# Block transposes on VectorE in place of TensorE transposes for six experts' tokens

## Chip, core and metric

The kernel runs on one core of one Trainium2 chip. The metric is the device time of one execution in microseconds, the lower the better. Of the core's engines five matter: TensorE (PE, matmuls, and PEld, its weight loads), VectorE (DVE), ScalarE (ACT), POOL, and SP, whose queue issues the loads of the weights. Each engine takes its instructions strictly in the order in which the program has them.

## The reference

```
state = alpha[t] * state + k[t] v[t]^T        # per batch (2) and head (8), 768 steps, 48 wide
y[t] = q[t] state                             # -> x, 1536 tokens x 384
# first layer: top-1 of 8 experts, capacity 384, F = 1024
x = gate * (relu(x_e @ w1[e]) @ w2[e])
# second layer: noisy top-2 of 8 experts, no capacity
for e in range(8):
    for k in range(2):
        mask = top2[:, k] == e
        h = relu(x[mask] @ moe2_w1[e])
        out[mask] += top2_w[mask, k] * (h @ moe2_w2[e])
```

All of it is in f32. An f32 product is made here from a high part and a rest of both factors, in three matmuls.

## The kernel before

A manual schedule writes every instruction out in the order of its engine. Sixteen jobs follow one another, one per expert: jobs 0 to 7 are the first layer, jobs 8 to 15 the second. Jobs 8 and 9 of the second layer are experts 0 and 1 (304 and 432 token places), jobs 10 to 15 the six others, called placed experts: which of them comes when is decided on the chip by their counts, and they have 432, 412, 400, 396, 384 and 384 places (CAPS). Their rows and weights are therefore addressed by a register.

A job n has two stages of eight steps f each. `hidden` (lines 600 to 615): per f six matmuls of the three 128-feature chunks of xh, the high part of the tokens (line 608), then three of xl, the rest (line 611); ScalarE and VectorE make h and its rest from PSUM (lines 613, 614). `second` (lines 619 to 637): per f nine matmuls (line 637) that build three output tiles py. Between them, at f = 2, 6 and 7 of `second`, stands `split_x` of the next job, one chunk d of its tokens each time: TensorE transposes the gathered rows (line 567, with the identity iw), ScalarE copies PSUM to xh (line 571), VectorE subtracts for xl (line 572). The stage `hidden` of the next job takes chunk d of xh with its matmuls 2d + 1 and 2d + 2.

`load_x` (line 551) gathers the rows of the next job on POOL's queue, each row of 394 f32: 384 features, then gate, token and others. They were put into the store xs2 by scatters at the end of the first layer.

The weights of the next job are loaded by SP (lines 490 for w1, 493 for w2), and split in sixteen parts q: ScalarE makes the high part (line 508), and the rest is a subtract with two SBUF inputs (line 509), which goes to POOL or to VectorE by a string, ENGS. In the second layer that string gives q = 11 and q = 14 to VectorE and the other fourteen to POOL; q = 8 to 15 stand between the steps f of `second`. (In job 9, q = 4 to 7 stand there too.)

At the end of a job ScalarE copies output tiles 0 and 2 to yT (line 813) and VectorE tile 1 (line 811); TensorE transposes yT back to rows after the next job's first f (line 821), these are weighted (lines 789, 791) and scattered by POOL into the output (line 157). Jobs 14 and 15 compute rows directly and have no yT.

Of the kernel before, what the change touches and what calls it, by code (L numbers as in the profile page):

```python
# [6 lines left out]
F32 = mybir.dt.float32  # L7
# [5 lines left out]
ALU = mybir.AluOpType  # L13
# [13 lines left out]
NF2 = 2  # L27
# [39 lines left out]
def body(tc, ap, cap, dbg=False, stop=False):  # L67
    nc = tc.nc
    V, A, G, PE = nc.vector, nc.scalar, nc.gpsimd, nc.tensor
    with ExitStack() as ctx:  # L70
# [124 lines left out]

        zt = []

        def zero_rows(store, e, n, r):

            nc.sync.dma_start(store[:E * R].rearrange("(e r) d -> r e d", e=E)[r:r + 128, e:e + n],  # L200
                              zt[0][:, None, :RW].to_broadcast([128, n, RW]))

        def zero_xs1():
            zero = s6([128, 1536])
# [5 lines left out]
        def zero_xs2():  # L210
            zero_rows(xs2, 0, 1, LOW3)
            zero_rows(xs2, 0, E, LOW2)

        def zero_out(i):
            nc.sync.dma_start(out[i * 512:(i + 1) * 512].rearrange("(p k) d -> p (k d)", p=128), zt[0][:, :4 * DM])
# [265 lines left out]
        def raw(n, i):  # L481
            if n >= len(jobs):
                return
            layer = jobs[n][0]
            e = expert(n, mybir.EngineType.SP)
            one = slice(e, e + 1) if place(n) is None else bass.ds(e, 1)
            w1, w2 = ap[f"w1_{layer}"][one], ap[f"w2_{layer}"][one]
            if i < 2:
                t = s6([128, ND, 512])
                nc.sync.dma_start(t, w1.rearrange("o (d p) f -> p (o d) f", p=128)[:, :, i * 512:(i + 1) * 512])  # L490
            else:
                t = s6([128, 4, DM])
                nc.sync.dma_start(t, w2.rearrange("o (f p) d -> p (o f) d", p=128)[:, (i - 2) * 4:(i - 1) * 4, :])
            raws[n, i] = t
# [27 lines left out]
            return hi[:, f % 4, :], lo[:, f % 4, :]  # L522


        xg, xsp = {}, {}

        def dims(n):

# [13 lines left out]
        def load_x(n, eng):  # L542
            layer, e = jobs[n]
            nt_, p, c = dims(n)
            store = (xs1, xs2)[layer - 1]
            g = sb([p, nt_, RW], "b6", 5)
            if place(n) is None:
                rows_ = store[e * R:e * R + nt_ * p]
            else:
                rows_ = store[bass.ds(expert(n, eng.engine) * R, nt_ * p), :]  # L550
            eng.dma_start(g, rows_.rearrange("(t p) d -> p t d", p=p))
            xg[n] = g
            xsp[n] = (xb([128, ND, c], F32R), xb([128, ND, c], F32R))

        def split_x(n, d):
            layer, e = jobs[n]
            nt_, p, c = dims(n)
            g, (xh, xl) = xg[n], xsp[n]
            ds = (d,)
            if layer == 1:  # L560
                if d == 2:
                    return
                ds = ((0, 1), (2,))[d]
            xp = pm()
            for k, d in enumerate(ds):
                for t, sl, r in tiles(n):
                    PE.transpose(xp[:, k * c + sl.start:k * c + sl.stop], g[:r, t, d * 128:(d + 1) * 128],  # L567
                                 ident[:r, :r])
            m = lambda x: x[:, ds[0]:ds[-1] + 1, :].rearrange("p d c -> p (d c)")
            w = len(ds) * c  # L570
            A.activation(m(xh), xp[:, :w], AF.Copy)  # L571
            V.tensor_tensor(m(xl), xp[:, :w], m(xh).bitcast(F32), op=ALU.subtract)  # L572
# [755 lines left out]
def prepare(i):  # L1328
# [13 lines left out]
    for (b, c0, n) in (a_ for ps_ in PARTS for a_ in ps_):  # L1342
# [11 lines left out]

    by_part = lambda x, n: x.reshape(n, 128, E).transpose(1, 0, 2)
    w2 = np.concatenate([by_part(i["moe2_w_gate"], ND), by_part(i["moe2_w_noise"], ND)], axis=2)
    few = np.concatenate([x.reshape(128, -1) for x in (wg1, w2, by_part(i["moe2_noise"], N // 128))], axis=1)

    return {
        "q": q[:, :HR], "k": k[:, :HR], "ks": of_pieces(k), "qs": of_pieces(q), "a": a[:, :HR], "few": few, "as": np.concatenate(pieces, axis=1),  # L1360
        "v": np.ascontiguousarray(i["v"].transpose(0, 2, 1, 3)).reshape(B, S, DM),
        "wgn": i["moe_w_gate"],
        "w1_1": i["moe_w1"], "w2_1": i["moe_w2"], "w1_2": i["moe2_w1"], "w2_2": i["moe2_w2"],
    }


# [15 lines left out]
```

## Time and profile before

| | us |
|---|---|
| median of 3 runs | 490.23 (489.21 to 491.54) |
| profiled execution, device time | 492.09 |
| its span | 490.2 |
| TensorE busy | 474.1 (97%) |
| VectorE busy | 308.4 (63%) |
| ScalarE busy | 262.6 (54%) |
| POOL busy | 319.9 (65%) |
| mean granted clock of TensorE | 0.993 |

The profile is of one execution; its device time lies 1.86 us over the median, and is 1.9 longer than its span. Busy shares are over all stages. The second layer takes the part of the span from about 267 on; job 9's `second` begins at 296.68, job 10's `hidden` at 311.93, and job 15's `hidden` at 456.56.

### The profile page before, as it was taken

How to read it: one execution, taken by the hardware profiler on the slowest of the kernel's cores; microseconds unless marked ns; L12 is line 12 of the kernel's file. 1: busy time of each engine (PE TensorE's matmuls, PEld its weight loads, DVE VectorE, ACT ScalarE, POOL GpSimd, SP SyncE). 2: the span in 40 equal slices, each digit the busy share in tenths (PEclk: the TensorE clock that was granted, in tenths of full speed). 3: DMA queues.
4: the chain of work that ended last, by engine and by line, in shares of the span. 5: the costliest groups of instructions: out<-in, count | busy, mean ns of one | idle time of the engine just before them, and what ended most of it. 6: DMA issues, size and time to landing. Idle time of an engine off the chain costs nothing.

```text
span 490.2 us, 9808 instructions
## 1 busy us (share of the span) xinstructions
PE 474.1 (97%) x3542; PEld 445.6 (91%) x3542; DVE 308.4 (63%) x856; ACT 262.6 (54%) x676; POOL 319.9 (65%) x400
## 2 busy tenths in 40 slices
PE   8899999999999999999999999999999999999993
PEld 4588888899999999999998799999999999999993
DVE  7989988557786786786863424735454362746540
ACT  3467787466666675675661356453535536354310
POOL 3434496565777777885865269695794949779322
PEclk9989999999999999999999999999999999999998
DMA  8953863699888868676733854482745847361133
GB/s 284 407 194 137 322 238 103 213 319 283 282 264 264 267 219 274 181 242 216 232 107 105 254 122 151 140 216 78 178 126 156 212 127 165 110 164 21 20 46 42
DMA packets 47797, 91.65 MB, mean 187 GB/s; under 512 B 4625, under 2 KB 29154, under 8 KB 47739
## 3 DMA queue, kind: packets, MB, share of 16 engines
q1 hardware_dynamic: 38090, 70.32, 43.2%
q0 software_dynamic: 9648, 20.61, 18.1%
q8 instruction: 30, 0.49, 0.4%
q14 instruction: 29, 0.23, 0.2%
HBM read 70.63 MB, written 20.28 MB: 185 GB/s over the span
## 4 chain that ended last, share of the span: by engine, by line
PE 68%; DVE 16%; DMA 4%; issue 4%; ACT 4%; POOL 3%; SPq 0%; POOLq 0%; DVEq 0%
PE py L637 28%; PE ph L608 18%; PE ph L611 9%; DMA xs<-b,m_si 3%; PE pm L567 2%; DVE s L509 2%; DVE s L236 2%; DVE h L614 2%; POOL xs L157 2%; PE pm L821 2%; DVE s L253 1%; DVE s L255 1%; PE pm L665 1%; DVE s L240 1%; PE pm L365 1%
## 5 line engine op out<-in xcount | busy, mean ns | idle before, releaser
L509 POOL TENSOR_TENSOR s<-s,s 128x384 fp32r<-128x384 f32 x175 | 184.6, 1263 | 50.1 <-ACT s L508 45.2
L637 PE MATMUL py<-h,s 128*128 128x240 f32 (+5 forms) x1008 | 154.3, 307 | 0.0
L637 PEld LDWEIGHTS py<-h,s 128*128 128x128 f32 x1008 | 142.7, 189 | 1.1
L608 PE MATMUL ph<-x,s 128*128 128x240 f32 (+6 forms) x768 | 136.0, 312 | 1.9 <-DVE h L614 0.9
L508 ACT ACTIVATE s<-s 128x384 fp32r<-128x384 f32 x256 | 123.1, 515 | 1.1 <-DMA s<-w 1.0
L608 PEld LDWEIGHTS ph<-x,s 128*128 128x128 f32 x768 | 115.5, 189 | 4.5 <-DVE h L614 2.5
L614 DVE SCALAR_TENSOR_TENSOR h<-ph,h 128x240 fp32r<-128x240 f32 (+6 forms) x128 | 61.1, 484 | 70.5 <-ACT h L613 63.8
L509 DVE TENSOR_TENSOR s<-s,s 128x384 fp32r<-128x384 f32 x81 | 88.3, 1111 | 3.4 <-ACT s L508 2.7
L613 ACT ACTIVATE h<-ph 128x240 fp32r<-128x240 f32 (+6 forms) x128 | 55.2, 432 | 59.9 <-PE ph L611 55.5
L611 PE MATMUL ph<-x,s 128*128 128x240 f32 (+6 forms) x384 | 76.6, 308 | 0.0
L157 POOL DMA_INDIRECT out<-b,m_ix x29 | 46.5, 1605 | 43.0 <-ACT b L789 23.0
L611 PEld LDWEIGHTS ph<-x,s 128*128 128x128 f32 x384 | 61.2, 189 | 0.4
L571 ACT ACTIVATE x<-pm 128x480 fp32r<-128x480 f32 (+7 forms) x38 | 18.6, 489 | 63.3 <-PE pm L567 63.3
L157 POOL DMA_INDIRECT xs<-b,m_si x32 | 32.9, 1028 | 16.4 <-DVE pm L746 11.4
L298 POOL TENSOR_SCALAR_AFFINE_SELECT h<-h 128x512 f32<-128x512 f32 x24 | 22.1, 942 | 30.8 <-ACT h L297 30.3
L572 DVE TENSOR_TENSOR x<-pm,x 128x480 fp32r<-128x480 f32 (+7 forms) x38 | 20.7, 550 | 27.6 <-ACT x L571 27.2
L637 PE MATMUL py<-s,h 128*128 128x384 f32 x144 | 26.5, 339 | 0.0
L637 PEld LDWEIGHTS py<-s,h 128*128 128x128 f32 x144 | 25.0, 188 | 0.0
L236 DVE TENSOR_TENSOR s<-s,s 112x256 f32<-112x256 f32 (+2 forms) x24 | 19.3, 824 | 1.6 <-DMA s<-qs 1.1
L567 PE MATMUL pm<-iw,b 108*128 108x108 f32 (+5 forms) x129 | 18.7, 260 | 0.8 <-DVE h L865 0.5
L155 POOL MEMSET spacer<- 1x1 f32 x74 | 18.8, 254 | 0.1
L169 PE MATMUL ph<-warm 128*128 128x512 bf16 x66 | 16.9, 415 | 1.5 <-POOL warm L164 1.5
(240 smaller groups left out, 553.9 us busy)
## 6 DMA issues: line engine op xcount, KB each, us to landing
s<-w SPq DMA_DIRECT2D x64, 768.0 KB, 5.7
xs<-s SPq DMA_DIRECT2D x2, 1576.0 KB, 6.5
out<-s SPq DMA_DIRECT2D x4, 768.0 KB, 8.2
b<-xs POOLq DMA_DIRECT2D x4, 664.9 KB
b<-xs POOLq DMA_DIRECT2D x7, 369.4 KB
s<-as SPq DMA_DIRECT2D x2, 780.5 KB
s<-ks SPq DMA_DIRECT2D x2, 768.0 KB, 9.0
s<-qs SPq DMA_DIRECT2D x2, 768.0 KB
```

What stands on the lines that cost most here:

```text
L157: st = G.indirect_dma_start(out=dst, out_offset=bass.IndirectOffsetOnAxis(ap=ix, axis=0), in_=src, in_offset=None, **kw)
L236: eng.tensor_tensor(o, src[:, h].rearrange("r (s j) -> r s j", j=64), x[:, h].rearrange("r (s j) -> r s j", j=64), op=ALU.mult)
L298: G.affine_select(a_, a_, pattern=[[0, 4], [1, 128]], compare_op=ALU.is_ge, fill=0.0, base=0, channel_multiplier=-1)
L508: A.activation(hi[sl], t[sl], AF.Copy)
L509: rest.append(lambda: (eng or V).tensor_tensor(lo[sl], t[sl], hi[sl].bitcast(F32), op=ALU.subtract))
L567: PE.transpose(xp[:, k * c + sl.start:k * c + sl.stop], g[:r, t, d * 128:(d + 1) * 128], ident[:r, :r])
L572: V.tensor_tensor(m(xl), xp[:, :w], m(xh).bitcast(F32), op=ALU.subtract)
L608: PE.matmul(p, w, x[:, d, :], start=(k == 0), stop=False)
L611: PE.matmul(p, w1_of(n, f, d)[0], xl[:, d, :], start=False, stop=(d == ND - 1))
L613: A.activation(hh, p, AF.Relu)
L614: V.scalar_tensor_tensor(hl, p, 0.0, hh.bitcast(F32), op0=ALU.max, op1=ALU.subtract)
L637: PE.matmul(out_, l, r, start=(f == 0 and k == 0), stop=(f == NF - 1 and k == 2))
```

## The change

For the six placed experts the features no longer come as whole rows. Four loads on SP's queue (line 570 of the changed kernel) bring blocks of 32 tokens by 96 features: block b of the features goes to partitions 32b to 32b + 31, so that token j of a group of 32 lies on partition 32b + j. VectorE then turns each chunk of 32 columns, 32 by 32 (line 583), into a tile y of 128 features by the tokens, rounded up to a multiple of 32. ScalarE makes xh from y (line 584), VectorE xl from y and xh (line 585), all in SBUF. Feature 96b + 32d + i becomes row 32b + i of chunk d, and the rows of the first weights are put in that order on the host (`by_block`, a new input w1_b). POOL's load (line 565) is left with the last ten columns. Rows of the store up to the next multiple of 32 are set to zero in the first layer. The order of the steps is left as it is: chunk d stands where chunk d stood. Line numbers shift: 490 and 493 become 491 and 494, 508 and 509 become 509 and 510, 608 and 611 become 635 and 638, 637 becomes 664, 811 and 813 become 838 and 840, 821 becomes 848.

```diff
--- before.py
+++ after.py
@@ -195,10 +195,10 @@
 
         zt = []
 
-        def zero_rows(store, e, n, r):
-
-            nc.sync.dma_start(store[:E * R].rearrange("(e r) d -> r e d", e=E)[r:r + 128, e:e + n],
-                              zt[0][:, None, :RW].to_broadcast([128, n, RW]))
+        def zero_rows(store, e, n, r, k=128):
+
+            nc.sync.dma_start(store[:E * R].rearrange("(e r) d -> r e d", e=E)[r:r + k, e:e + n],
+                              zt[0][:k, None, :RW].to_broadcast([k, n, RW]))
 
         def zero_xs1():
             zero = s6([128, 1536])
@@ -210,6 +210,7 @@
         def zero_xs2():
             zero_rows(xs2, 0, 1, LOW3)
             zero_rows(xs2, 0, E, LOW2)
+            zero_rows(xs2, NF2, E - NF2, C2, -C2 % 32)
 
         def zero_out(i):
             nc.sync.dma_start(out[i * 512:(i + 1) * 512].rearrange("(p k) d -> p (k d)", p=128), zt[0][:, :4 * DM])
@@ -484,7 +485,7 @@
             layer = jobs[n][0]
             e = expert(n, mybir.EngineType.SP)
             one = slice(e, e + 1) if place(n) is None else bass.ds(e, 1)
-            w1, w2 = ap[f"w1_{layer}"][one], ap[f"w2_{layer}"][one]
+            w1, w2 = ap[f"w1_{layer}" if place(n) is None else "w1_b"][one], ap[f"w2_{layer}"][one]
             if i < 2:
                 t = s6([128, ND, 512])
                 nc.sync.dma_start(t, w1.rearrange("o (d p) f -> p (o d) f", p=128)[:, :, i * 512:(i + 1) * 512])
@@ -522,7 +523,18 @@
             return hi[:, f % 4, :], lo[:, f % 4, :]
 
 
-        xg, xsp = {}, {}
+        xg, xsp, xr_ = {}, {}, {}
+
+        class few_of:
+
+            def __init__(self, x):
+                self.x, self.shape = x, (*x.shape[:2], RW)
+
+            def __getitem__(self, at):
+                p, t, c = at
+                if isinstance(c, slice):
+                    return self.x[p, t, c.start - DM:None if c.stop is None else c.stop - DM]
+                return self.x[p, t, c - DM]
 
         def dims(n):
 
@@ -543,12 +555,20 @@
             layer, e = jobs[n]
             nt_, p, c = dims(n)
             store = (xs1, xs2)[layer - 1]
-            g = sb([p, nt_, RW], "b6", 5)
             if place(n) is None:
-                rows_ = store[e * R:e * R + nt_ * p]
+                g = sb([p, nt_, RW], "b6", 5)
+                eng.dma_start(g, store[e * R:e * R + nt_ * p].rearrange("(t p) d -> p t d", p=p))
             else:
-                rows_ = store[bass.ds(expert(n, eng.engine) * R, nt_ * p), :]
-            eng.dma_start(g, rows_.rearrange("(t p) d -> p t d", p=p))
+                nb = -(-c // 32)
+                t6 = sb([128, nb * ND * 32 + nt_ * (RW - DM)], "b6", 5)
+                g = few_of(t6[:p, nb * ND * 32:].rearrange("p (t d) -> p t d", t=nt_))
+                eng.dma_start(g[:, :, DM:], store[bass.ds(expert(n, eng.engine) * R, nt_ * p), :].rearrange(
+                    "(t p) d -> p t d", p=p)[:, :, DM:])
+                x = xr_[n] = t6[:, :nb * ND * 32].rearrange("p (t d) -> p t d", t=nb)
+                rows_ = store[bass.ds(expert(n, mybir.EngineType.SP) * R, nb * 32), :]
+                for b in range(4):
+                    nc.sync.dma_start(x[b * 32:b * 32 + 32], rows_.rearrange("(t j) d -> j t d", j=32)[
+                        :, :, b * ND * 32:(b + 1) * ND * 32])
             xg[n] = g
             xsp[n] = (xb([128, ND, c], F32R), xb([128, ND, c], F32R))
 
@@ -557,6 +577,13 @@
             nt_, p, c = dims(n)
             g, (xh, xl) = xg[n], xsp[n]
             ds = (d,)
+            if place(n) is not None:
+                x = xr_[n][:, :, d * 32:d * 32 + 32]
+                y = hb([128, x.shape[1] * 32])
+                V.transpose(y.rearrange("p (t j) -> p t j", j=32), x)
+                A.activation(xh[:, d, :], y[:, :c], AF.Copy)
+                V.tensor_tensor(xl[:, d, :], y[:, :c], xh[:, d, :].bitcast(F32), op=ALU.subtract)
+                return
             if layer == 1:
                 if d == 2:
                     return
@@ -1354,13 +1381,14 @@
 
     by_part = lambda x, n: x.reshape(n, 128, E).transpose(1, 0, 2)
     w2 = np.concatenate([by_part(i["moe2_w_gate"], ND), by_part(i["moe2_w_noise"], ND)], axis=2)
+    by_block = i["moe2_w1"].reshape(E, 4, ND, 32, F).transpose(0, 2, 1, 3, 4).reshape(E, DM, F)
     few = np.concatenate([x.reshape(128, -1) for x in (wg1, w2, by_part(i["moe2_noise"], N // 128))], axis=1)
 
     return {
         "q": q[:, :HR], "k": k[:, :HR], "ks": of_pieces(k), "qs": of_pieces(q), "a": a[:, :HR], "few": few, "as": np.concatenate(pieces, axis=1),
         "v": np.ascontiguousarray(i["v"].transpose(0, 2, 1, 3)).reshape(B, S, DM),
         "wgn": i["moe_w_gate"],
-        "w1_1": i["moe_w1"], "w2_1": i["moe_w2"], "w1_2": i["moe2_w1"], "w2_2": i["moe2_w2"],
+        "w1_1": i["moe_w1"], "w2_1": i["moe_w2"], "w1_2": i["moe2_w1"], "w1_b": by_block, "w2_2": i["moe2_w2"],
     }
```

On VectorE, in job 9's `second`, behind the rests of its hidden layer, there stood before (x_4401 is xl of job 10, pm a transposed chunk, s weights of job 10):

```order
L572 TENSOR_TENSOR x_4401<-pm_4566,x_4400 128x432
L509 TENSOR_TENSOR s_846_4547<-s_821_4436,s_845_4546 128x384
L509 TENSOR_TENSOR s_848_4551<-s_777_4228,s_847_4550 128x3x128
L572 TENSOR_TENSOR x_4401<-pm_4628,x_4400 128x432
L572 TENSOR_TENSOR x_4401<-pm_4648,x_4400 128x432
L509 TENSOR_TENSOR s_852_4615<-s_838_4510,s_851_4614 128x384
L811 COPY b_856_4666<-py_4537 128x432
```

And there stands now, in the changed kernel (h_4571, h_4630 and h_4647 are the tiles y, b_810 the loaded blocks):

```order
L583 STREAM_TRANSPOSE h_4571<-b_810_4396 128x448
L585 TENSOR_TENSOR x_4406<-h_4571,x_4405 128x432
L510 TENSOR_TENSOR s_846_4552<-s_821_4441,s_845_4551 128x384
L510 TENSOR_TENSOR s_848_4556<-s_777_4229,s_847_4555 128x3x128
L583 STREAM_TRANSPOSE h_4630<-b_810_4396 128x448
L585 TENSOR_TENSOR x_4406<-h_4630,x_4405 128x432
L583 STREAM_TRANSPOSE h_4647<-b_810_4396 128x448
L585 TENSOR_TENSOR x_4406<-h_4647,x_4405 128x432
L510 TENSOR_TENSOR s_852_4617<-s_838_4515,s_851_4616 128x384
L838 COPY b_856_4662<-py_4542 128x432
```

Three transposes have come in, one ahead of each subtract for xl, and the subtract's first input has gone from PSUM (pm) to SBUF (h). Both L510 of q = 7 and q = 11 still stand behind the first subtract.

On TensorE, in the same place ahead of f = 7 of that `second`, there stood before (iw is the identity):

```order
L637 MATMUL py_4541<-h_4505,s_829_4471 128x432
L567 MATMUL pm_4648<-iw_83,b_810_4395 128x108 x4
L637 MATMUL py_4533<-h_4525,s_828_4470 128x432
L637 MATMUL py_4533<-h_4526,s_828_4470 128x432
L637 MATMUL py_4533<-h_4525,s_829_4471 128x432
```

The row of line 567 is gone after. At the end of the same `second` and the start of job 10's `hidden` there stands now:

```order
L664 MATMUL py_4546<-h_4530,s_829_4476 128x432
L635 MATMUL ph_4673<-x_4405,s_830_4479 128x432
L635 MATMUL ph_4673<-x_4405,s_831_4480 128x432
L635 MATMUL ph_4673<-x_4405,s_830_4479 128x432
L635 MATMUL ph_4673<-x_4405,s_831_4480 128x432
L635 MATMUL ph_4673<-x_4405,s_830_4479 128x432
L635 MATMUL ph_4673<-x_4405,s_831_4480 128x432
L638 MATMUL ph_4673<-x_4406,s_830_4479 128x432 x3
L848 MATMUL pm_4688<-iw_83,b_856_4662 108x128 x3
```

There is nothing left between the last matmul with w2 and the first of `hidden`, nor further ahead, that reads the tokens of job 10; the matmuls themselves stand as before. On SP's queue the four loads of line 570 stand behind the two w1 loads of the same job and ahead of its two w2 loads, for each of the six jobs.

## Rows read from the trace of the kernel before

**Rows 1.** The page, part 1: busy time, share and count of each engine.
```profile
PE 474.1 (97%) x3542; PEld 445.6 (91%) x3542; DVE 308.4 (63%) x856; ACT 262.6 (54%) x676; POOL 319.9 (65%) x400
```

**Rows 2.** Windows: stretch, length, busy time (instructions) by engine, granted clock, DMA share, GB/s.
```profile
core 0: us, PE busy (x) PEld busy (x) DVE busy (x) ACT busy (x) POOL busy (x), PEclk, DMA share, GB/s
312.00:342.70 30.70, 30.70 (x169) 29.18 (x168) 13.86 (x23) 14.38 (x31) 21.38 (x25) 1.00 0.64 173
```

**Rows 3.** Chain of waits, 296 to 457: shares by line, then pieces (start, us, what).
```profile
by line: PE py L637 50.2%; PE ph L608 28.0%; PE ph L611 14.1%; PE pm L821 4.1%; PE pm L567 3.9%
...
300.20 0.37 PE pm L567 x4
...
311.93 1.18 PE ph L608 x6
...
429.08 1.05 PE ph L608 x6
...
454.65 0.33 PE pm L567 x3
```

**Rows 4.** Groups by line and form, whole run: busy us, mean ns, idle before.
```profile
L572 DVE TENSOR_TENSOR x<-pm,x 128x432 fp32r<-128x432 f32 x6 | 3.4, 599 | 3.4 <-ACT x L571 3.3
L240 DVE TENSOR_TENSOR_SCAN s<-s,s 112x512 f32<-112x512 f32 x2 | 2.4, 1218 | 0.0
L571 ACT ACTIVATE x<-pm 128x432 fp32r<-128x432 f32 x6 | 3.2, 530 | 6.9 <-PE pm L567 6.9
L508 ACT ACTIVATE s<-s 128x384 fp32r<-128x384 f32 x256 | 123.1, 515 | 1.1 <-DMA s<-w 1.0
```

**Rows 5.** Timeline of POOL, job 9: start, us, instruction, idle before it, releaser.
```profile
291.43 18.74 POOL L509 TENSOR_TENSOR s<-s,s 128x384 fp32r<-128x384 f32 x19
```

**Rows 6.** Timeline of VectorE in the same stretch of job 9, and in job 10.
```profile
301.18 0.61 DVE L572 TENSOR_TENSOR x<-pm,x 128x432 fp32r<-128x432 f32 x1 [3.29 <-ACT x L571]
302.47 8.59 DVE L509 TENSOR_TENSOR s<-s,s 128x384 fp32r<-128x384 f32 x2 [0.69 <-POOL s L509]
...
332.71 3.92 DVE L509 TENSOR_TENSOR s<-s,s 128x384 fp32r<-128x384 f32 x1 [0.24 <-ACT s L508]
```

**Rows 7.** Timelines at the ends of jobs 10 and 13, POOL and VectorE.
```profile
341.95 1.01 POOL L509 TENSOR_TENSOR s<-s,s 128x384 fp32r<-128x384 f32 x1 [5.75 <-ACT s L508]
...
342.00 1.38 DVE L509 TENSOR_TENSOR s<-s,s 128x384 fp32r<-128x384 f32 x1
...
428.50 1.45 POOL L509 TENSOR_TENSOR s<-s,s 128x384 fp32r<-128x384 f32 x1 [3.32 <-ACT s L508]
...
428.52 0.55 DVE L509 TENSOR_TENSOR s<-s,s 128x384 fp32r<-128x384 f32 x1
...
429.46 0.51 DVE L766 TENSOR_SCALAR m_iz<-b 108x4 f32<-108x4 f32 x1
430.01 0.16 DVE L767 TENSOR_TENSOR m_iz<-m_iz,tro 108x4 f32<-108x4 f32 x1
```

**Rows 8.** Timeline of POOL, its streams in jobs 13 and 14.
```profile
415.71 9.47 POOL L509 TENSOR_TENSOR s<-s,s 128x384 fp32r<-128x384 f32 x9
...
443.74 9.25 POOL L509 TENSOR_TENSOR s<-s,s 128x384 fp32r<-128x384 f32 x9
```

**Rows 9.** Timeline of SP's queue, job 8: loads of job 10's weights.
```profile
267.88 1.13 SPq L490 DMA_DIRECT2D s<-w  x2
272.70 7.74 SPq L493 DMA_DIRECT2D s<-w  x2
```

**Rows 10.** Timelines of POOL and VectorE in the first layer.
```profile
179.39 3.28 POOL L509 TENSOR_TENSOR s<-s,s 128x384 fp32r<-128x384 f32 x3 [0.34 <-ACT s L508]
...
180.90 2.19 DVE L509 TENSOR_TENSOR s<-s,s 128x384 fp32r<-128x384 f32 x2
```

**Rows 11.** Timeline of TensorE at 24 us, and windows as in group 2.
```profile
24.15 0.57 PE L283 MATMUL py<-iw,s 112*128 112x112 f32 x4 [1.41 <-DVE s L236]
...
26.00:29.30 3.30, 3.30 (x18) 2.78 (x17) 3.23 (x4) 1.88 (x7) 2.72 (x3) 0.50 0.15 56
```

## The prediction

> **What bounds the kernel now.** I read the busy line first: TensorE works 97% of the span [rows 1]. That alone names no limit, so I cut the stretch of the second layer into windows: from 312.00 to 342.70 TensorE is busy for all 30.70 us at a granted clock of 1.00, VectorE for 13.86 and POOL for 21.38 [rows 2]. The chain of waits over jobs 9 to 14 consists of TensorE alone, and its line of shares gives the transposes of line 567, the only TensorE work that the change takes out there, 3.9% [rows 3]. So a transpose removed is time won, provided that what replaces it is ready before TensorE asks for it. The question is therefore how late VectorE is at the end of each `second`, and for that I read the timelines of POOL and VectorE side by side.
>
> **What is removed.** Six placed experts times three chunks are 18 pieces of line 567, the first of 0.37 us at 300.20 and the last of 0.33 at 454.65 [rows 3]. By width: 3 x 0.37 (432 tokens) + 0.36 + 0.36 + 0.35 (412) + 3 x 0.35 (400) + 3 x 0.34 (396) + 6 x 0.33 (384) = 6.2 us. This is the most the change can win.
>
> **What is added on VectorE and ScalarE.** Per chunk a block transpose T (line 583) comes new; the copy on ScalarE and the subtract S stay, but read the SBUF tile y instead of PSUM. The trace has no block transpose. From below, T costs what VectorE takes for one pass over 128x432, 0.60 us [rows 4]; from above, what a scan takes, whose 1.22 us for 512 columns [rows 4] is 1.07 for 448. I take 0.61: T makes one independent pass, as the subtract does, where a scan carries a value from column to column. That y is read from SBUF by ScalarE costs nothing extra: the copy takes 530 ns from PSUM for 432 columns, the weights' copy 515 from SBUF for 384 [rows 4], the same per column within a few per cent.
>
> **The wait that appears.** S now has two SBUF inputs, as the weights' subtract L509 has. In job 9 POOL runs L509 without a gap from 291.43 to 310.17 [rows 5]. VectorE's L509, asked for at 302.47, ends with a second one at 311.06 [rows 6]: two operations of 0.55 us each took 8.59, that is, the first got no turn before POOL's stream ended; in job 10 one alone took 3.92 [rows 6]. The L572 before it, with one input in PSUM, took 0.61 in the midst of the same stream [rows 6]. So after the change S for chunk 0 waits for the end of POOL's stream, P, in every job; and since VectorE takes its work in order, L510 (the old L509) and T and S for chunks 1 and 2 stand behind it, where before only chunks 1 and 2 stood behind L509, with their copies still to come from TensorE.
>
> From P on, VectorE and ScalarE take turns. Steps, with 0.08 us overlap of successive VectorE operations and 0.04 for a handover: S0 ends at P + 0.47; each L510 behind it adds 0.47 (two in job 9, one later); T1 0.53; the ScalarE copy 0.61; S1 0.64; T2 0.53; copy 0.61; S2 0.64.
>
> Job 9: P = 310.17, hence copy 1 at 312.72, copy 2 at 314.50, S2 at 315.14. Without its three transposes TensorE would start `hidden` of the next job 1.11 earlier than 311.93 [rows 3], at 310.82. Its six matmuls with xh take 1.18 [rows 3], so that the third, which wants chunk 1, is due at 311.21: it stops for 1.6 us; the fifth, due 0.4 later, stops for 1.4. The nine matmuls end at 315.56 instead of 312.59. Then TensorE wants the transposes of line 821 (848 after), which need VectorE's copy of yT chunk 1, and that stands behind S2 and the last L510. L510 takes 0.47 and the copy 0.51, so 316.12, a stall of 3.6 in all, if L510 gets its turn at once. But POOL asks for its own last L510 within 0.1 us of it, and when POOL came first by a little, VectorE's L509 waited: 1.38 instead of 0.55 at 342.00, where POOL had started at 341.95 [rows 7]. That adds 0.83: a stall of **4.4 us**.
>
> Job 13, the other kind: POOL's stream from 415.71 lasts 9.47, so P = 425.18 [rows 8], with one L510 and 384 columns (T 0.47, copy 0.58, S 0.60 by the same shares): copy 1 at 427.17, copy 2 at 428.82, S2 at 429.42. `hidden` would start 3 x 0.33 before 429.08 [rows 3], at 428.08, want copy 2 at 428.78 and end at 429.66: no stop worth counting. The yT copy, however, is ready at 430.38 (VectorE first) or 431.2 (POOL first): 0.7 or **1.5**. There the two had asked together at 428.5, and both outcomes of such a race are in the trace: here VectorE took 0.55 and POOL 1.45 [rows 7].
>
> The same sum for the other four, the last of whose streams ends at 443.74 + 9.25 = 452.99 [rows 8]: job 10 none, job 11 0 or 0.25, job 12 0.06 or 0.88, job 14 0.3 (no yT copy follows it). The race is nearly even in time, but POOL's request comes 0.03 to 0.09 us before VectorE's by my steps, so I take POOL first: 4.4 + 0 + 0.25 + 0.9 + 1.5 + 0.3 = 7.4. If VectorE wins every race it is 4.65.
>
> **The transfers.** The four x transfers per job (line 570) go to SP's queue between the w1 and the w2 loads. For job 10 that is between 269.0 and 272.70 [rows 9], 28 us before T0 can use them. I cost them at nothing: the cover is that distance, and the w2 loads behind them, wanted in the next `second`, have as much. POOL's L551, now ten columns wide, issues the same number of rows and stays as it is. The one more store of zeros goes to SP's queue in the first layer, ahead of nothing that the chain waits for, and I cost it at nothing too.
>
> **Sum.** Profiled execution 492.09: minus 6.2 plus 7.4 is 493.3, and on the median of the runs shown, 490.23, which is 1.86 lower, **491.4**. 0.5% is 2.45 us, about what a measurement here can tell from no change: faster means under 487.8, slower over 492.7.
>
> **Rivals.**
> *VectorE gets in between POOL's operations.* In the first layer POOL's three L509 from 179.39 and VectorE's two from 180.90 ended within half a us of each other [rows 10]: neither starved the other. If S gets its turn at P minus several us, all of S0 to S2 is done before `hidden` and the whole 6.2 is won: 484.0. What speaks against it is the 8.59 us of [rows 6]; the stream in the first layer is three operations long and begins after a wait, the one in job 9 is nineteen long. The Trainium skill, "SBUF — State Buffer", section "SBUF: two separate sides", says that the shared ports are held for one whole instruction by whichever starts first, for a DVE operation with two SBUF inputs against a GpSimd one. By that rule alone S would wait one POOL operation and the time would be that of this rival; the first layer's row agrees with it, the 8.59 us does not. 12%.
>
> *VectorE wins the last race.* 6.2 against 4.65: 488.6. For it: the outcome at 428.52 [rows 7]. 20%.
>
> *The clock falls after the stop in job 9.* TensorE stood idle 1.4 us before 24.15, and from 26.00 to 29.30 the granted clock was 0.50 [rows 11]. The two stops of 1.6 and 1.4 in job 9 are of that size. Half speed over 3.3 us costs 1.65: 493.1. Against it: only one such stop in the trace is followed so closely, and VectorE's wait has matmuls between the two. 12%.
>
> *T is dear, or is itself held.* This is the one that decides for slower. T at 1.07 us adds 0.46 twice to every job's chain: stalls 5.4 + 0 + 1.2 + 1.8 + 2.3 + 1.2 = 11.9, hence 495.9; it ends over 492.7 from a T of about 0.8 on. If T0, with one SBUF input, also waits for POOL, about 1.3 us come on each job, some 13.7 in all, and 497.7. A row for it: L766, which reads SBUF alone, took 0.51 at 429.46, while POOL was working, the L767 behind it, of the same size, 0.16 [rows 7]. The Trainium skill, "Vector Engine (DVE) Microarchitecture Reference", on its transpose mode, gives one element per cycle and lane, which would put T at the lower end; no run here shows that yet. 16%.
>
> **Chances.** Main case 37%, the rivals 12, 20, 12 and 16, other mishaps 3. Faster by over 0.5%: the first rival and a third of the second, 18%. Slower: the last rival, most of the clock's, a little of the main case's upper side, 31%. Same: 51%. The main case alone holds 489.5 to 493. The range leaves out the first rival at one end and the upper half of the last at the other: 486.5 to 494.8.
>
> **What the profile after would show.** No L567 piece in jobs 9 to 14, and T of 0.6 us on line 583. If I am right, the first L585 of each job lasts until POOL's stream ends (some 5 to 9 us long), `hidden` after job 9 waits for ScalarE's line 584 twice, and line 848 waits for line 838 in jobs 9, 12 and 13. I am wrong in the main step if L585 lasts 0.6 throughout (then TensorE has no gap and 6 us are won), and in the size if T lasts 1 us or more, or if the granted clock is under 1.00 behind 311.

## The result, and the profile after

| | before | after |
|---|---|---|
| median of 15 runs, us | 489.51 (488.49 to 491.54) | 492.55 (491.07 to 496.56) |
| ratio, 95% interval | | 1.0064 (1.0044 to 1.0085) |
| profiled execution: device time, span | 492.09, 490.2 | 492.17, 490.5 |

The change costs 0.64%, some 3 us: a little slower, 1.15 us above the forecast of 491.4 and inside its range. (Each ratio goes by all runs of the two kernels on the same chip, not by the medians.) As a change, the forecast was +1.2 us on the three runs of before that were shown; against the fifteen above +3.0 was measured. By the forecast's own line of 0.5% that is slower, which it gave 31%, and not the same, which it gave 51%.

The two profiled spans differ by 0.3 alone, because in the profile of before job 9's `second` begins 3.4 us later (296.52 against 293.07, first matmul). The shift isn't of the change: it stands at the end of the first layer already (259.41 at line 460, 256.07 at line 461 after), two runs below on the changed kernel have it too (e3_warm begins job 9's `second` at 295.49, e5_psum_first at 296.11), and the kernel before with one copy moved (the control below) begins it at 293.41. So stages are compared, from the first matmul of one `second` to that of the next, and times by the medians.

The medians hold one more difference that no stage shows. From job 15's `second` to the end of the span it takes 21.0 to 21.4 us in the profiles of before, after, e1_psum, e3_warm, e4_t2, e8_before_yt and e11_best_t2, and 22.3 to 22.6 in the other six; the last scatter stands 13.95 us behind its start in before and after, e1_psum and e2_first alike, so that the difference lies behind it. Its cause is open. A difference of under 2 us between two medians is therefore told from the stages too.

The page's lines after that answer to [rows 1] and to L572 in [rows 4]; in the second, busy us, mean ns, then the idle time before:

```profile
PE 470.1 (96%) x3473; PEld 439.6 (90%) x3476; DVE 335.9 (68%) x874; ACT 263.9 (54%) x676; POOL 320.6 (65%) x400
...
L585 DVE TENSOR_TENSOR x<-h,x 128x384 fp32r<-128x384 f32 (+4 forms) x18 | 51.0, 2833 | 12.0 <-ACT x L584 12.0
```

TensorE works 4 us less, and line 585 takes 2.8 us on average where the subtract from PSUM took 0.6. What TensorE waits for stands in the rows of its timeline with idle time before them, jobs 9 to 14 (start, us, instruction, idle before it and releaser); before the change there was none:

```profile
311.11 1.09 PE L635 MATMUL ph<-x,s 128*128 128x432 f32 x2 [3.41 <-ACT x L584]
312.90 1.09 PE L635 MATMUL ph<-x,s 128*128 128x432 f32 x2 [0.70 <-ACT x L584]
...
374.45 0.43 PE L848 MATMUL pm<-iw,b 128*108 128x128 f32 x2 [0.31 <-DVE b L838]
...
403.12 0.43 PE L848 MATMUL pm<-iw,b 128*108 128x128 f32 x2 [1.01 <-DVE b L838]
...
431.15 0.43 PE L848 MATMUL pm<-iw,b 128*108 128x128 f32 x2 [0.29 <-DVE b L838]
...
457.57 0.61 PE L635 MATMUL ph<-x,s 128*128 128x384 f32 x2 [0.67 <-ACT x L584]
```

Job 9 has two stops for ScalarE's copies, jobs 11 to 13 one each for the copy of yT, job 14 one for ScalarE. POOL's timeline around job 9, which answers to [rows 5], and VectorE's, which answers to [rows 6]:

```profile
279.66 1.59 POOL L157 DMA_INDIRECT out<-h,m_ix  x1 [8.98 <-ACT h L816]
...
286.52 1.60 POOL L157 DMA_INDIRECT out<-b,m_ix  x1 [5.24 <-DVE h L641]
...
288.74 19.75 POOL L510 TENSOR_TENSOR s<-s,s 128x384 fp32r<-128x384 f32 x20
313.33 1.02 POOL L510 TENSOR_TENSOR s<-s,s 128x384 fp32r<-128x384 f32 x1 [4.84 <-ACT s L509]
```

```profile
296.77 12.20 DVE L585 TENSOR_TENSOR x<-h,x 128x432 fp32r<-128x432 f32 x1 [1.78 <-ACT x L584]
308.89 1.01 DVE L510 TENSOR_TENSOR s<-s,s 128x384 fp32r<-128x384 f32 x2
309.83 0.63 DVE L583 STREAM_TRANSPOSE h<-b 128x448 f32<-128x448 f32 x1
311.08 0.61 DVE L585 TENSOR_TENSOR x<-h,x 128x432 fp32r<-128x432 f32 x1 [0.63 <-ACT x L584]
311.61 0.64 DVE L583 STREAM_TRANSPOSE h<-b 128x448 f32<-128x448 f32 x1
312.88 0.61 DVE L585 TENSOR_TENSOR x<-h,x 128x432 fp32r<-128x432 f32 x1 [0.63 <-ACT x L584]
313.40 1.37 DVE L510 TENSOR_TENSOR s<-s,s 128x384 fp32r<-128x384 f32 x1
314.69 0.59 DVE L838 COPY b<-py 128x432 f32<-128x432 f32 x1
```

POOL's stream has 20 operations in both kernels: the row of [rows 5] lacks the first, which begins at 290.45 (its whole row stands with the transfers below); its end is the same. The first subtract, asked for at 296.77, ends at 308.97, half a us behind POOL's stream (288.74 + 19.75 = 308.49). Behind it stand the two L510, and only then comes T1, whose copy TensorE has been waiting for since 307.70. The last L510 takes 1.37, since POOL was first by 0.07. TensorE's clock, windows as in [rows 2]:

```profile
core 0: us, PE busy (x) PEld busy (x) DVE busy (x) ACT busy (x) POOL busy (x), PEclk, DMA share, GB/s
311.00:316.00 5.00, 4.13 (x11) 2.86 (x12) 4.18 (x10) 2.81 (x7) 1.04 (x2) 0.50 0.53 159
316.00:320.00 4.00, 4.00 (x20) 3.72 (x19) 1.07 (x2) 1.94 (x4) 3.05 (x4) 0.87 0.81 211
```

Stage lengths, worked out from the first matmuls of each `second` in TensorE's timeline (us); the forecast is that of before, less the transposes, plus the stall:

| job | before | forecast | after |
|---|---|---|---|
| 9 | 30.75 | 34.07 | 36.73 |
| 10 | 30.08 | 29.01 | 28.92 |
| 11 | 29.02 | 28.22 | 28.40 |
| 12 | 28.60 | 28.46 | 28.60 |
| 13 | 27.88 | 28.38 | 27.74 |
| 14 | 26.11 | 25.45 | 26.06 |
| sum | 172.44 | 173.59 | 176.45 |

Job 9 is 2.7 over the forecast; the rest together is 0.2 over.

### The profile page after: what moved, and what is told of

Its sections match the earlier page's. It is cut to its first block, busy times and chain, and to the rows that moved or that the text cites. A ratio compares the mean times of both kernels' runs of the same rounds, so it can differ in the third digit from the quotient of the medians.

```text
span 490.5 us, 9808 instructions
## 1 busy us (share of the span) xinstructions
PE 470.1 (96%) x3473; PEld 439.6 (90%) x3476; DVE 335.9 (68%) x874; ACT 263.9 (54%) x676; POOL 320.6 (65%) x400
## 4 chain that ended last, share of the span: by engine, by line
PE 53%; issue 16%; DVE 12%; POOL 10%; ACT 6%; DMA 1%; POOLq 0%; DVEq 0%; SPq 0%; ACTq 0%
PE py L664 15%; PE ph L635 12%; PE ph L638 6%; POOL out L157 4%; POOL s L510 4%; DVE s L510 4%; PE ph L169 3%; DVE h L641 3%; PE ph L290 2%; ACT x L584 2%; PE pm L366 2%; DVE h L583 2%; PE py L343 2%; PE py L337 2%; PE py L317 2%
## 5 line engine op out<-in xcount | busy, mean ns | idle before, releaser
L510 POOL TENSOR_TENSOR s<-s,s 128x384 fp32r<-128x384 f32 x175 | 184.9, 1268 | 52.8 <-ACT s L509 46.7
L664 PE MATMUL py<-h,s 128*128 128x240 f32 (+5 forms) x1008 | 150.6, 306 | 0.0
L635 PE MATMUL ph<-x,s 128*128 128x240 f32 (+6 forms) x768 | 138.6, 315 | 5.8 <-ACT x L584 4.8
L638 PE MATMUL ph<-x,s 128*128 128x240 f32 (+6 forms) x384 | 77.1, 309 | 0.0
L510 DVE TENSOR_TENSOR s<-s,s 128x384 fp32r<-128x384 f32 x81 | 65.7, 833 | 1.4 <-ACT s L509 1.1
L585 DVE TENSOR_TENSOR x<-h,x 128x384 fp32r<-128x384 f32 (+4 forms) x18 | 51.0, 2833 | 12.0 <-ACT x L584 12.0
L299 POOL TENSOR_SCALAR_AFFINE_SELECT h<-h 128x512 f32<-128x512 f32 x24 | 22.3, 955 | 27.5 <-ACT h L298 27.5
L584 ACT ACTIVATE x<-h 128x384 fp32r<-128x384 f32 (+4 forms) x18 | 9.7, 539 | 51.0 <-DVE h L583 51.0
L598 ACT ACTIVATE x<-pm 128x480 fp32r<-128x480 f32 (+3 forms) x20 | 9.5, 474 | 17.8 <-PE pm L594 17.8
```

Source lines behind the costliest of these rows:

```text
L299: G.affine_select(a_, a_, pattern=[[0, 4], [1, 128]], compare_op=ALU.is_ge, fill=0.0, base=0, channel_multiplier=-1)
L510: rest.append(lambda: (eng or V).tensor_tensor(lo[sl], t[sl], hi[sl].bitcast(F32), op=ALU.subtract))
L584: A.activation(xh[:, d, :], y[:, :c], AF.Copy)
L585: V.tensor_tensor(xl[:, d, :], y[:, :c], xh[:, d, :].bitcast(F32), op=ALU.subtract)
L635: PE.matmul(p, w, x[:, d, :], start=(k == 0), stop=False)
L638: PE.matmul(p, w1_of(n, f, d)[0], xl[:, d, :], start=False, stop=(d == ND - 1))
```

## The experiments

Theory A was the forecast's mechanism: the subtract for xl, with two SBUF inputs, gets no turn while POOL works through its stream, and chunks 1 and 2 stand behind it. Theory B put the time down to the small transfers or to the transposes' own time on VectorE.

**Input of the subtract (e1_psum).** Everything else as in the changed kernel:

```diff
-                y = hb([128, x.shape[1] * 32])
+                y = pm()[:, :x.shape[1] * 32]
```

> The changed kernel with one edit: the block transpose writes its tile y into PSUM instead of SBUF, so that the subtract for xl has one input in PSUM and one in SBUF, as before the change. Block transposes, the four transfers per job and the reordered weights stay. Theory A (the subtract with two SBUF inputs gets no turn until POOL's stream ends, and the next two transposes and copies queue behind it): line 585 takes about 0.6 us each time instead of up to 12.2, TensorE has no gap in jobs 9 to 14, the granted clock stays at 1.00 behind 311, and the whole 6.2 us of TensorE's transposes is won: 489.5 - 6.2 = 483.3, between 482 and 485. Rival B (the many small transfers on SP's queue, or the transposes' own time on VectorE, make the chunks late): the gaps stay, 490 or more.

Measured 491.14, ratio 1.0031 (1.0008 to 1.0054): 1.4 us better than the changed kernel by the medians, with intervals that overlap, and 1.9 by the six stages (174.57 against 176.45). That is far from 483.3; the expectation was missed. The group of line 585 on VectorE (durations min/median/max in ns), VectorE's first L510 in job 9, and TensorE's stops there:

```profile
L585 DVE TENSOR_TENSOR x<-pm,x x18: 556/572/608, 296.5 to 455.5; 128x384 fp32r<-128x384 f32 x6, 128x432 fp32r<-128x432 f32 x3, 128x412 fp32r<-128x412 f32 x3, 128x400 fp32r<-128x400 f32 x3
...
297.83 11.07 DVE L510 TENSOR_TENSOR s<-s,s 128x384 fp32r<-128x384 f32 x2 [0.69 <-ACT s L509]
...
310.08 0.81 PE L635 MATMUL ph<-x,s 128*128 128x432 f32 x2 [2.58 <-ACT x L584]
311.85 1.09 PE L635 MATMUL ph<-x,s 128*128 128x432 f32 x2 [0.96 <-ACT x L584]
```

Half of theory A held. The subtract is free (0.6 us throughout), but now the L510 behind it is held (two take 11.07, the first of them 10.6), and T1 still stands behind that. The new SBUF input is only a part of the cause that I took it for: the old subtract with two SBUF inputs, which stood there before, does the same. What the change made worse is the order: chunk 1 and 2 used to reach ScalarE from TensorE, past VectorE's queue.

**Order (e2_first).** y in SBUF as in the changed kernel, but at f = 2:

```diff
+                if d == 0:
+                    ...
+                    for k in range(ND):
+                        ...
+                        V.transpose(y.rearrange("p (t j) -> p t j", j=32), x)
+                        A.activation(xh[:, k, :], y[:, :c], AF.Copy)
+                        ys[n].append(y)
+                V.tensor_tensor(xl[:, d, :], ys[n][d][:, :c], xh[:, d, :].bitcast(F32), op=ALU.subtract)
```

> The changed kernel with another order: at f = 2 all three block transposes and all three copies on ScalarE stand ahead of the first subtract; the subtracts stay where they were and still have two SBUF inputs. Theory A: xh is never late, but the subtracts still wait for the end of POOL's stream. From that end P on, S0, the L510 behind it, S1 and S2 take 0.5 us each, so that S2 is ready at P + 2.4 in job 9 and at P + 2.0 in the others, where it was P + 4.6 or more. Jobs 11 to 14, which waited 0.3 to 1.0, wait no longer (2.3 us won); job 9, where P came 1.35 after the start of the next hidden stage, still stops for 2 to 4 us, now at the matmuls with xl and at line 848. About 489.5, between 486 and 491, with the first line 585 of a job still 5 to 12 us long. Rival B: the order changes nothing that it names, 492 or more.

Measured 488.44, 0.9965 (0.9943 to 0.9987): 4.1 us better than the changed kernel by the medians, as expected, and 5.9 by the stages (170.54). VectorE in job 9:

```profile
297.25 12.34 DVE L589 TENSOR_TENSOR x<-h,x 128x432 fp32r<-128x432 f32 x1 [0.72 <-ACT x L587]
309.51 1.01 DVE L510 TENSOR_TENSOR s<-s,s 128x384 fp32r<-128x384 f32 x2
310.44 1.11 DVE L589 TENSOR_TENSOR x<-h,x 128x432 fp32r<-128x432 f32 x2
```

The subtract is held for 12.34 us, and xl and yT are late in job 9 (TensorE stops 0.68, 0.99 and 0.41); jobs 10 to 14 have no stop.

**Both (e5_psum_first).** y in PSUM, and T0, T1, S0, T2, S1, S2 with their copies at f = 2, ahead of the first L510.

```diff
+                if d:
+                    return
+                for k in (0, 1, -1, 2, -2, -3):
+                    if k >= 0:
+                        ...
+                        ys.append(pm()[:, :x.shape[1] * 32])
+                        V.transpose(ys[k].rearrange("p (t j) -> p t j", j=32), x)
+                        A.activation(xh[:, k, :], ys[k][:, :c], AF.Copy)
+                    else:
+                        k = -1 - k
+                        V.tensor_tensor(xl[:, k, :], ys[k][:, :c], xh[:, k, :].bitcast(F32), op=ALU.subtract)
```

> The changed kernel with y in PSUM, and all three transposes, copies and subtracts of a job at f = 2, ahead of the first L510 on VectorE (order T0, T1, S0, T2, S1, S2). Theory A2, as it stands after the first runs: what is late are the transposes and copies of chunks 1 and 2, because on VectorE they stand behind operations with two SBUF inputs that wait for POOL's stream; it makes no difference whether that is the subtract for xl or the L510 behind it. Then here xh and xl are ready by about 300 in job 9 and never late; what is left is the copy of yT (line 838), which still stands behind three L510 in job 9: 1.5 to 2 us late there and nowhere else. 489.3 - 6.2 + 1.7 + up to 0.8 for the clock = 485 to 486. Rival C (the transposes on VectorE or the small transfers cost time by themselves): a gap at xh stays and the time is over 488.

Measured 484.84, 0.9915 (0.9883 to 0.9947), about as expected. The profiled execution is the longest of the six, 489.75, some 3 us of it the late first layer named above. TensorE's only row with a stop in it from 296 to 457:

```profile
314.21 0.43 PE L855 MATMUL pm<-iw,b 128*108 128x128 f32 x2 [1.99 <-DVE b L845]
```

Line 855 there is the transposition of yT (848), line 845 VectorE's copy, behind three L510 that POOL holds.

**The last copy too (e6_yt).** In addition, yT on ScalarE alone:

```diff
-                if d == 1:
-                    V.tensor_copy(yT[:, d, :], yp[d][:, :c])
-                else:
-                    A.activation(yT[:, d, :], yp[d][:, :c], AF.Copy)
+                A.activation(yT[:, d, :], yp[d][:, :c], AF.Copy)
```

> As the run before it in this list (y in PSUM, all three chunks at f = 2), and in all jobs the copy of yT tile 1 goes to ScalarE behind tile 0 instead of VectorE. Theory A2: nothing that TensorE waits for stands behind an operation held by POOL any more, so TensorE has no gap from 296 to 457 and the whole 6.2 us is won: 489.3 - 6.2 = 483.1, between 482.3 and 484.5. Rival C: a gap stays, 486 or more.

Measured 483.19, 0.9874 (0.9848 to 0.99), as expected: the whole of what the transposes cost. Windows (length, busy by engine, clock, DMA share, GB/s), and VectorE's L510:

```profile
296.00:311.00 15.00, 15.00 (x80) 14.36 (x79) 12.98 (x8) 8.38 (x20) 14.16 (x16) 1.00 0.66 188
311.00:330.00 19.00, 19.00 (x102) 18.11 (x101) 9.40 (x22) 9.72 (x21) 16.21 (x19) 1.00 0.69 161
330.00:440.00 110.00, 110.00 (x623) 108.91 (x623) 57.56 (x93) 58.56 (x129) 84.89 (x97) 1.00 0.63 147
...
300.63 10.89 DVE L510 TENSOR_TENSOR s<-s,s 128x384 fp32r<-128x384 f32 x3 [0.69 <-ACT s L509]
```

TensorE is busy without a gap. VectorE's three L510 are held for 10.89 us as ever, but nothing that TensorE wants stands behind them.

**Control (e8_before_yt).** The same edit of yT (lines 810 to 813) on the kernel before.

```diff
-                if d == 1:
-                    V.tensor_copy(yT[:, d, :], yp[d][:, :c])
-                else:
-                    A.activation(yT[:, d, :], yp[d][:, :c], AF.Copy)
+                A.activation(yT[:, d, :], yp[d][:, :c], AF.Copy)
```

> Control: the kernel before with one edit, the copy of yT tile 1 on ScalarE instead of VectorE. There TensorE has no gap in jobs 9 to 14 to begin with, so nothing is to be won: 489.3, within 1 us. If this alone is faster by over 1 us, the gain of the run with the same edit on the changed kernel isn't that of the block transposes alone.

Measured 488.90, 0.9998 (0.9979 to 1.0016): the copy alone gains nothing. The gain is that of the block transposes.

**Subtracts in SBUF, rest as in the best (e9_sbuf_first_yt).** The order at f = 2 is T0, T1, T2, S0, S1, S2, so that two things differ from the best run, the place of y and, a little, the order.

```diff
+                if d == 0:
+                    ...
+                    for k in range(ND):
+                        ...
+                        y = hb([128, x.shape[1] * 32])
+                        ...
+                    for k in range(ND):
+                        V.tensor_tensor(xl[:, k, :], ys[n][k][:, :c], xh[:, k, :].bitcast(F32), op=ALU.subtract)
```

> As the best run so far (all three chunks at f = 2, the copy of yT on ScalarE), but with y in SBUF again, so that the three subtracts have two SBUF inputs; the transposes and copies stand ahead of them. Theory A2: xh is in time; the subtracts wait for POOL's stream, which ends about 1.5 us after job 10's hidden stage starts, and S2 is ready 1.5 us behind that, where 1.6 would be due from the stage's start: a stop of 1.0 to 1.8 us in job 9, none in the other jobs. 483.2 + 1.4 + up to 0.8 for the clock = 484.5 to 485.5. If the subtract's second SBUF input were the whole cause, jobs 11 to 14 would keep their gaps and the time would be over 488.

Measured 484.89, 0.9916 (0.9888 to 0.9944), as expected. VectorE's three subtracts, and TensorE's only stop:

```profile
296.66 13.65 DVE L590 TENSOR_TENSOR x<-h,x 128x432 fp32r<-128x432 f32 x3 [0.72 <-ACT x L587]
...
309.33 1.50 PE L643 MATMUL ph<-x,s 128*128 128x432 f32 x3 [0.96 <-DVE x L590]
```

By the stages, the input's place is worth about 1.8 us with the right order (167.73 here, 165.98 in the best run) and 1.9 with the old one. The order alone is worth more, 5.9.

**Transposes doubled, in the changed kernel and in the best (e4_t2, e11_best_t2).** Each transpose is done twice into the same tile.

```diff
-                V.transpose(y.rearrange("p (t j) -> p t j", j=32), x)
+                for _ in range(2):
+                    V.transpose(y.rearrange("p (t j) -> p t j", j=32), x)
```

> The changed kernel with each block transpose done twice into the same tile: 36 instead of 18. Theory A: T1 and T2 stand in the row from POOL's end to the end of the job, so that jobs 9, 12, 13, 14 take 1.1 us more each and job 11 about as much: 4 to 5.5 us slower than the changed kernel, 496.5 to 498. If transposes were hidden by the wait and only the transfers or the weights' order cost time, it would be 492.5 as before.

Measured 500.37, 1.0214 (1.0175 to 1.0253): 7.8 us more than the changed kernel, more than expected. The stages of jobs 9 to 13 grow by 0.4 to 1.3, about what the second T1 and T2 take, but job 14's by 2.8: its stop comes to 1.63, and there the clock falls too (windows as above):

```profile
463.99 0.62 PE L636 MATMUL ph<-x,s 128*128 128x384 f32 x2 [1.63 <-ACT x L585]
...
464.00:468.00 4.00, 4.00 (x14) 4.00 (x15) 2.84 (x7) 1.32 (x3) 2.22 (x3) 0.57 0.00 0
```

> The run with y in PSUM, all three chunks at f = 2 and the copy of yT on ScalarE, with each block transpose done twice. Theory A2: the transposes now stand ahead of everything that POOL holds and 10 us ahead of their use, so that their time doesn't count: 483.2, within 1 us, where the same doubling made the changed kernel 7.8 us slower. If a transpose's own time counts, 486 or more.

Measured 481.64, 0.9834 (0.9804 to 0.9864), 1.6 us under the expectation. From job 9's `second` to job 15's it takes 165.98 us, as in the run with single transposes (165.98). The difference lies behind that stretch: 21.16 us from there to the end of the span, 22.60 in the run with single transposes. VectorE at f = 2:

```profile
294.85 2.56 DVE L589 STREAM_TRANSPOSE pm<-b 128x448 f32<-128x448 f32 x4
```

So a transpose's time counts behind the held operations and not ahead of them.

**The transfers (e7_big, e10_late_x).** POOL's scatter ahead of job 9's stream stands 6.55 us ahead of the stage in the changed kernel (286.52 to 293.07) and 8.29 before (288.23 to 296.52); it waits for the late tokens' scatter to land, 6.86 us where it was 5.12. POOL's rows before the change:

```profile
288.23 1.60 POOL L157 DMA_INDIRECT out<-b,m_ix  x1 [3.50 <-DVE h L614]
...
290.45 19.71 POOL L509 TENSOR_TENSOR s<-s,s 128x384 fp32r<-128x384 f32 x20
```

The first run changes what the four loads read:

```diff
-                    nc.sync.dma_start(x[b * 32:b * 32 + 32], rows_.rearrange("(t j) d -> j t d", j=32)[
-                        :, :, b * ND * 32:(b + 1) * ND * 32])
+                    nc.sync.dma_start(t6[b * 32:b * 32 + 32, :nb * ND * 32], rows_.rearrange("(j t) d -> j (t d)", j=32)[
+                        :, b * nb * ND * 32:(b + 1) * nb * ND * 32])
```

> The changed kernel with the same bytes in the four loads of line 570, but read as one piece of up to 5376 bytes for each partition instead of pieces of 384 bytes; the tokens that the six placed experts see are therefore not theirs, and everything behind the loads is as in the changed kernel. Theory D: the small pieces keep the DMA engines busy from 272 to 283, so that the late tokens' scatter lands 1.7 us later than before the change, POOL's fourth scatter and with it the stream of job 9 start 1.7 us later against TensorE, and the stop in job 9 is 6.4 us instead of 4.7. With large pieces the scatter of POOL ahead of that stream stands about 8.3 us ahead of job 9's second stage again instead of 6.6, and the time falls by 1.5 to 2.5 us to 490 to 491. If the pieces cost nothing (as predicted), the distance stays 6.6 and the time 492.5.

Measured 493.47, 1.0083 (1.0054 to 1.0112), no better than with small pieces, so the expectation was missed. POOL's timeline:

```profile
280.78 1.59 POOL L157 DMA_INDIRECT out<-h,m_ix  x1 [10.33 <-issue]
...
285.73 1.60 POOL L157 DMA_INDIRECT out<-b,m_ix  x1 [3.32 <-DVE h L641]
...
287.95 19.72 POOL L510 TENSOR_TENSOR s<-s,s 128x384 fp32r<-128x384 f32 x20
```

The wait for that scatter is short again (4.95). But the late tokens' scatter itself went out later, 12.10 us ahead of the stage (292.88) instead of 13.41, and in this run the scatter ahead of it landed late, at 279.58 instead of 276.67. So the stream starts 4.93 us ahead of the stage, where it was 4.33 with small pieces and 6.07 before the change. The large pieces shift most of the delay to an earlier scatter, and the six stages take as long as with small ones (176.38 and 176.45): the size of the pieces is worth nothing here. The Trainium skill, "DMA: Bandwidth & Descriptors", section "Specifications", asks for 512 bytes or more in a piece for full rate; no run here shows a gain in time from that.

And the loads' place, small pieces again:

```diff
+                def blocks(q):
+                    ...
+                if n == E + 2:
+                    late_x.append(blocks)
+                else:
+                    blocks(nc.sync)
...
+                if f == 3 and late_x:
+                    late_x.pop()(nc.scalar)
```

> The changed kernel with one edit: the four loads of job 10's blocks are issued by ScalarE behind step f = 3 of job 9's hidden stage, some 15 us later than on SP's queue; the other five jobs' loads stay. Theory D2, as it stands after the run with large pieces: it is the 0.69 MB in front of the w2 loads and of the late tokens' scatter, not the size of the pieces, that puts POOL's last scatter ahead of job 9's stream later against TensorE. With the loads behind that scatter the distance from POOL's scatter to job 9's second stage goes back from 6.6 towards 8.3 us, the stop in job 9 shrinks by 1 to 1.7 us, and the time falls to 490.5 to 491.5. If the distance stays, the loads are not what moves it. ScalarE's own time for issuing could take some of it back.

Measured 492.68, 1.0055 (1.0033 to 1.0077). The loads went out at 287.43, 21 us later than on SP's queue. POOL's timeline, TensorE's stops in job 9, whose stage begins at 293.49, and the piece of the chain of waits for its second transposition of yT:

```profile
285.07 1.60 POOL L157 DMA_INDIRECT out<-b,m_ix  x1 [3.37 <-DVE h L647]
...
287.30 19.73 POOL L510 TENSOR_TENSOR s<-s,s 128x384 fp32r<-128x384 f32 x20
...
309.65 0.66 PE L641 MATMUL ph<-x,s 128*128 128x432 f32 x2 [1.52 <-ACT x L590]
311.44 1.09 PE L641 MATMUL ph<-x,s 128*128 128x432 f32 x2 [1.14 <-ACT x L590]
...
313.88 0.67 PE pm L854 x2
```

The distance is back at 8.42 and the stops are 2.66 instead of 4.11: the loads' place is what moved POOL's stream. The time did not follow, and that expectation was missed. Job 9's stage is only 0.93 shorter (35.80), since more of the slow matmuls now lie behind the stops: the clock is at 0.55 from 315 to 318, where it is 0.87 from 316 to 320 in the changed kernel. The median shows nothing even of that; in the profile the end of the span is 1.6 us longer (22.58 against 21.00).

**The clock (e3_warm).** 14 matmuls without use ahead of job 10's `hidden`:

```diff
+            if n == E + 2:
+                warm(14)
             for f in range(NF):
                 hidden(n, f)
```

> The changed kernel with 14 idle matmuls (128x512 bf16, on a tile of zeros, result unused) ahead of the first matmul of job 10's hidden stage, about 3.1 us of TensorE work where TensorE stopped for 3.4 us. Theory A with the clock: the stop costs twice, 4.1 us as a gap and about 3 as half clock from 311 to 316.5; with the gap filled the granted clock stays at 1.00 and some 2.5 to 3 us come back: 489.5 to 490. If the clock is not lowered by the stop but by something else, the time stays at 492.5 or rises by up to what the fill is too long in runs whose stop is shorter.

Measured 492.72, 1.004 (1.0018 to 1.0061); missed. Job 9's stage takes 35.60, 1.1 us less than in the changed kernel. Its clock over job 9's end, its second transposition of yT and the next `second`; and the piece of the chain of waits in the changed kernel that answers to the second:

```profile
315.00:318.00 3.00, 1.92 (x10) 1.54 (x11) 2.90 (x8) 1.82 (x5) 1.05 (x2) 1.00 0.35 130
...
317.41 0.43 PE L848 MATMUL pm<-iw,b 128*108 128x128 f32 x2 [1.08 <-DVE b L838]
...
331.09 2.11 PE L664 MATMUL py<-h,s 128*128 128x432 f32 x10
```

```profile
315.34 0.67 PE pm L848 x2
```

The clock stays at 1.00 when the long stop is filled, though stops of 1.13 and 1.08 are left, so it is the long stop that lowers it. But from that transposition to the next `second` it takes 13.68 us here (317.41 to 331.09) and 14.46 in the changed kernel (315.34 to 329.80): the low clock costs 0.8 us there, not 3. Most of the slow matmuls lie between the stops, where TensorE would wait for VectorE anyway.

## Why the prediction was right, and where it was not

**Removed.** 6.2 us, right within 0.3: without stops the six jobs take 165.98 instead of 172.44, 6.5 less, and the median falls by 5.7.

**T's price.** 0.61 taken; measured (group of line 583, durations min/median/max in ns):

```profile
L583 DVE STREAM_TRANSPOSE h<-b x18: 564/598/639, 294.4 to 456.4; 128x416 f32<-128x416 f32 x9, 128x384 f32<-128x384 f32 x6, 128x448 f32<-128x448 f32 x3
```

The Trainium skill, "Vector Engine (DVE) Microarchitecture Reference", section 3.8, has one element per cycle and lane: the trace agrees as far as it goes, with 0.57 us on average for 384 columns and 0.64 for 448, no dearer than the subtract. T itself was not held by POOL: T0, at 294.35 in the middle of the stream, took 0.64.

**The chain from POOL's end.** Forecast P + 6.77 to the copy of yT (316.94 - 310.17); TensorE went on at 315.34, P + 6.85, with POOL ahead of VectorE in the last race, as taken.

**The cause.** The mechanism was right, its origin half wrong. I put the wait down to the subtract's new SBUF input. The runs show two parts. One is the order, chunks 1 and 2 behind VectorE operations that POOL holds: mending it alone gives back 4.1 us by the medians, 5.9 by the stages. The other is the new input: mending it alone gives 1.4 and 1.9. Either alone leaves something that TensorE wants behind a held operation, xl and the copy of yT or chunks 1 and 2, for the L510 between them is held in either case. Both together, with the copy of yT on ScalarE, leave no stop.

**The size in job 9.** 4.4 forecast. Job 10's `hidden` was due to end its first step at 308.91 (307.14 + 1.77), and TensorE went on with the transposes of yT at 315.34: 6.4. The step that failed is "I cost them at nothing" of the transfers. The four loads of job 10 stand ahead of the w2 loads and of the late tokens' scatter, and POOL's stream ends 1.35 us behind the start of `hidden` instead of 0.65 ahead of it. With the loads later that came back: there the same sum is 4.5 (from 307.57 + 1.77 = 309.34 to 313.88), so the chain from P was right and its start was not. To this the fall of the clock adds 0.8: the clock's rival did occur, at half its price of 1.65. With the loads later it costs 1.7 (15.41 us from that transposition to the next `second`, 13.68 at full clock), which is why the time did not come back.

**Jobs 10 to 14.** Forecast stalls 0, 0.25, 0.9, 1.5, 0.3; by the table 0, 0.4, 1.0, 0.85, 0.9. In job 13 VectorE won the race.

**The other rivals.** "VectorE gets in between" did not happen: the first subtract waited through some twelve POOL operations. By the Trainium skill, "SBUF — State Buffer", section "SBUF: two separate sides", the ports are held for one whole instruction; the trace differs, 12.20 us held by a stream of operations of about 1 us. "T is dear" fell with T's 0.60; by the prediction's own steps it would have ended over 492.7 from a T of 0.74 on, not 0.8.

The nearness of 491.4 to 492.55 is partly luck. As a change, +1.2 us was forecast, and +4.0 was measured in the stages, +3.0 in the medians; nearly all that was missing is job 9's 2.7 (2.0 for the stream's place, 0.8 for the clock). The three runs of before that the sum stood on had a median 0.7 above that of the fifteen, which brought the two times closer.

## What to carry to other kernels

Before moving work to an engine off the critical path, read what stands ahead of it in that engine's order and whether that can be held by another engine: T cost 0.6 us, and T1 stood behind a wait of 12. The same block transposes cost 0.6% behind two held operations and won 1.3% ahead of them, with their result in PSUM and the last copy on ScalarE. A load that is early for its user can still be late for others: it pushed a scatter on which another engine's stream waited.

## What the runs showed that I had not expected

- VectorE's L510 starved as long behind POOL's stream with every input the same as before (10.6 us in the run with y in PSUM): the wait needs no change, only something behind it.
- With stops of 3.4 and 0.7 us the granted clock was 0.50 from 310.3 to 317.0, yet that cost only 0.8 us; with stops of 1.5 and 1.1 it was 0.50 from 311.0 to 317.6 and cost 1.7, so that of 1.9 us of shorter wait 0.9 was won.
- Four loads of 0.69 MB, over 20 us ahead of their use, moved another engine's stream by 1.7 us against TensorE.
